# A fused retention and FFN kernel: attention units in token-pair layout, with 512-byte loads and a block-diagonal state

## The chip, the cores and the metric

The kernel runs on one core of one Trainium2 chip. The metric is the time of one execution in microseconds (us), as the device measures it. Each kernel was run several times, and one of those executions was profiled. The chips of different calls differ a little (the kernel before had medians from 327.8 to 329.8 us), so kernels are compared by ratios to runs of the kernel before on the same chip.

Engines are called PE (TensorE), PEld (its weight loads), DVE (VectorE), ACT (ScalarE), POOL (GpSimd) and SP (SyncE). SPq, ACTq and POOLq are the DMA issues of those engines.

## The reference, cut to what matters

```python
# q, k, v: (8 batches, 8 heads, 576 tokens, 64) float32; w_in (512, 2048), w_out (2048, 512)
scores = q @ k^T / 8
ret = scores * gamma_h ** (pos_q - pos_k)        # 0 where pos_k > pos_q, one gamma per head
x = (ret @ v) as (4608 tokens, 512)              # heads side by side
h = x @ w_in
g = where(h > 0, h, exp(min(h, 0)) - 1)
out = g @ w_out                                  # (4608, 512) float32
```

## The kernel before

A *unit* is 128 tokens with all eight heads; there are 36 units, nine to a pair of batches (`R = 9`). Attention is computed unit by unit. Inside a unit it is quadratic (scores, mask, AV); what earlier units of the batch contribute comes through a running state (the sum of k^T v, called `state`, and its product with q, called `inter`). The decay is folded into the factors `gk` (for v) and `gx` (for the result). The FFN works in groups of up to 512 tokens. A *slot* is one step of its stream, that is, one call of `ffn1` or `ffn2` (`ffn2` holds the matmuls with w_out). From unit 4 on, PE mixes attention units into the stream of FFN matmuls.

The parts that the change and the argument touch:

```python
def load(u, after=None):                       # one DMA of 256 KB for each of q, k, v
    ...
    for p0, b, s0, n in place(u):              # one piece of 128 tokens, or two of 64
        for dst, src in ((qk[p0:p0+n, 0], q), (qk[p0:p0+n, 1], k), (vv[p0:p0+n], v)):
            nc.sync.dma_start(dst, src[b, :, s0:s0+n, :].rearrange("h p d -> p h d"))

def state(u):                                  # own PSUM tile "st", accumulates over units
    ...
    nc.tensor.matmul(st[i*D:(i+1)*D, hp], kns[u][rows, 1, h*D:(h+1)*D], vns[u][rows, h], ...)

def state_out(u):                              # bf16 copy of the state: ACT alone
    s = ppool.tile([P, HP, D], BF16, name="sb", tag="sb")
    nc.scalar.copy(s, sts[0])

def inter(u): ...                              # 8 matmuls in 64x64 mode
def intra(u): ...                              # 8 matmuls in 128x64 mode (AV)
def stretch(u):  # one unit inside the FFN: scores(u+1), inter, state, intra, masks, put_x, state_out

def ffn1(g, ft):                               # ph = x w_in; e = exp(ph) on ACT;
    ...                                        # m = (e - 1) on POOL; g = min(max(ph,0), m) on DVE,
    late.append((slot[0], gt_, ph, m, ...))    # three slots later

# ... startup: units 0 to 3, then w_in and w_out are triggered from POOL ...
for ft in range(NFT):
    ffn1(0, ft, ...)
    if ft == 5:
        load(4, nc.vector)                     # loads of units 4 to 11
        for u in range(5, 12):
            load(u)
```

From unit 12 on, q and k are transposed by a DMA transpose that SP issues; before that PE transposes them. Full stores of the first three FFN groups are issued by ACT, later ones by SP.

Of the kernel before, what the change touches and what calls it, by code (L numbers as in the profile page):

```python
# [9 lines left out]
FP32 = mybir.dt.float32  # L10
BF16 = mybir.dt.bfloat16
I32 = mybir.dt.int32
# [5 lines left out]
def kernel(  # L18
# [9 lines left out]
    nc = tc.nc  # L28
# [18 lines left out]
    def place(u):  # L47

        pair, r = divmod(u, R)
        if r < 4:  # L50
            return [(0, 2 * pair, P * r, P)]
        if r == 4:
            return [(0, 2 * pair, 4 * P, 64), (64, 2 * pair + 1, 0, 64)]
        return [(0, 2 * pair + 1, 64 + P * (r - 5), P)]
# [17 lines left out]
    ps_st = ctx.enter_context(tc.tile_pool(name="ps_st", bufs=1, space=PSUM))  # L72
# [4 lines left out]
    def load(u, after=None):  # L77

        qk = raw.tile([P, 2, H, D], FP32, name="rqk", tag="rqk")
        vv = raw.tile([P, H, D], FP32, name="rv", tag="rv")  # L80
        if after is not None:
            after.memset(qk[0:1, 0, 0, 0:1], 0.0)
        for p0, b, s0, n in place(u):
            for dst, src in ((qk[p0 : p0 + n, 0], q), (qk[p0 : p0 + n, 1], k), (vv[p0 : p0 + n], v)):
                nc.sync.dma_start(dst, src[b, :, s0 : s0 + n, :].rearrange("h p d -> p h d"))  # L85
        raws[u] = (qk, vv)
# [16 lines left out]
    for u in range(4):  # L103
        load(u)
# [6 lines left out]
    lgk = const.tile([P, H], FP32, name="lgk")  # L111
    for h in range(H):
        nc.vector.memset(lgk[:, h : h + 1], -lg[h])
# [7 lines left out]
    pk_i = const.tile([P, R], I32, name="pk_i")  # L121
    nc.gpsimd.iota(pk_i[:, 0:4], pattern=[[P, 4]], base=-MID, channel_multiplier=1)
    nc.gpsimd.iota(pk_i[0:64, 4:5], pattern=[[0, 1]], base=4 * P - MID, channel_multiplier=1)
    nc.gpsimd.iota(pk_i[64:P, 4:5], pattern=[[0, 1]], base=-MID, channel_multiplier=1)
    nc.gpsimd.iota(pk_i[:, 5:9], pattern=[[P, 4]], base=64 - MID, channel_multiplier=1)
# [4 lines left out]
    mask = const.tile([P, 2, P], BF16, name="mask")  # L130
    nc.vector.memset(mask, 1.0)
    for m in range(2):
        nc.gpsimd.affine_select(
            out=mask[:, m], in_=mask[:, m], compare_op=ALU.is_ge, fill=0.0,
            base=0, pattern=[[1, P]], channel_multiplier=-1,
        )
    nc.vector.memset(mask[0:64, 1, 64:P], 0.0)

    pk = const.tile([P, R], FP32, name="pk")
# [3 lines left out]
    ek = const.tile([P, R, H], FP32, name="ek")  # L143
    nc.vector.tensor_tensor(
        ek,
        pk.unsqueeze(2).to_broadcast([P, R, H]),
        lgk.unsqueeze(1).to_broadcast([P, R, H]),
        ALU.mult,
    )
    gk = const.tile([P, R, H], FP32, name="gk")  # L150
    nc.scalar.activation(gk, ek, AF.Exp)
# [8 lines left out]
    qkTs, kns, vns, scs, pts, os_, sbs, sts = {}, {}, {}, {}, {}, {}, {}, {}  # L160

    def cast(u, *engs):

        rqk, _ = raws[u]
        n = nat.tile([P, 2, H * D], BF16, name="qkn", tag="qkn")
        src = rqk.rearrange("p c h d -> p c (h d)")
        if len(engs) == 1:
            engs[0](n, src)  # L168
        else:
            for c in range(2):  # L170
                engs[c](n[:, c], src[:, c])  # L171
        kns[u] = n

    def scale_v(u):
        _, rv = raws[u]
        n = nat.tile([P, H, D], BF16, name="vn", tag="vn")
        nc.gpsimd.tensor_tensor(  # L177
            n, rv, gk[:, u % R].unsqueeze(2).to_broadcast([P, H, D]), ALU.mult
        )
        vns[u] = n  # L180

    def turn(u, bank=None):
        t = tpool.tile([P, 2, HP, P], BF16, name="qkT", tag="qkT")
        n = kns[u]
        if u < PE_TURNED:
            pool, tag = bank or (ps_s, "sc")
            ps = pool.tile([P, 2, HP, P], BF16, name="tr", tag=tag)
            for c in range(2):
                for hp in range(HP):
                    nc.tensor.transpose(ps[:, c, hp], n[:, c, hp * P : (hp + 1) * P], ident)  # L190
            nc.vector.tensor_copy(t[:, 0], ps[:, 0])  # L191
            nc.scalar.copy(t[:, 1], ps[:, 1])  # L192
        else:
            nc.sync.dma_start_transpose(
                t.rearrange("p c h t -> p (c h) t"), n.rearrange("p c f -> p (c f)")
            )
        qkTs[u] = t

    def scores(u):
        t = qkTs[u]  # L200
        sc = ps_s.tile([P, 2, HP, P], FP32, name="sc", tag="sc")
        for hp in range(HP):
            for j in range(2):
                for i in range(2):
                    r = slice(i * D, (i + 1) * D)
                    nc.tensor.matmul(  # L206
                        sc[j * 64 : (j + 1) * 64, i, hp], t[r, 1, hp, j * 64 : (j + 1) * 64], t[r, 0, hp],
                        start=(hp == 0), stop=(hp == HP - 1), skip_group_check=True,
                    )
        scs[u] = sc  # L210

    def masks(u):
        pt = ppool.tile([P, 2, HP, P], BF16, name="pt", tag="pt")
        m = mask[:, 1 if u % R == 4 else 0]
        nc.vector.tensor_tensor(  # L215
            pt.rearrange("p i h t -> p (i h) t"), scs[u].rearrange("p i h t -> p (i h) t"),
            m.unsqueeze(1).to_broadcast([P, 2 * HP, P]), ALU.mult,
        )
        pts[u] = pt

    def inter(u):

        o = ps_o.tile([P, HP, P], FP32, name="o", tag="o")
        os_[u] = o
        r = u % R
        if r == 0:
            return
        n = 64 if r == 4 else P
        for hp in range(HP):
            for i in range(2):  # L230
                rows = slice(i * D, (i + 1) * D)
                nc.tensor.matmul(  # L232
                    o[rows, hp, :n], sbs[u][rows, hp], qkTs[u][rows, 0, hp, :n],
                    start=(hp == 0), stop=False, skip_group_check=True,
                )

    def state(u):

        r = u % R
        if r == 8:  # L240
            return
        if r in (0, 4):
            sts[0] = ps_st.tile([P, HP, D], FP32, name="st", tag="st")
        st = sts[0]
        rows = slice(64, P) if r == 4 else slice(0, P)
        for hp in range(HP):
            for i in range(2):
                h = 2 * hp + i
                nc.tensor.matmul(  # L249
                    st[i * D : (i + 1) * D, hp], kns[u][rows, 1, h * D : (h + 1) * D], vns[u][rows, h],  # L250
                    start=(hp == 0 and r in (0, 4)), stop=(r in (3, 7)), skip_group_check=True,
                )

    def state_out(u):
        if u % R == 8:
            return
        s = ppool.tile([P, HP, D], BF16, name="sb", tag="sb")
        nc.scalar.copy(s, sts[0])  # L258
        sbs[u + 1] = s

    def intra(u):
        o = os_[u]
        for hp in range(HP):
            for i in range(2):
                h = 2 * hp + i
                nc.tensor.matmul(  # L266
                    o[i * D : (i + 1) * D, hp], vns[u][:, h], pts[u][:, i, hp],
                    start=(u % R == 0 and hp == 0), stop=(hp == HP - 1), skip_group_check=True,
                )
# [3 lines left out]
    def put_x(u):  # L273
        g, i = group_of[u]
        if i == 0:
            xts[g] = xpool.tile([P, KJ, 512], BF16, name="xt", tag="xt")
        r = u % R
        s0 = P * r if r < 5 else 64 + P * (r - 5)
        nc.vector.tensor_tensor(  # L279
            xts[g][:, :, i * P : (i + 1) * P], os_[u], gx[:, :, s0 : s0 + P], ALU.mult  # L280
        )

    def stretch(u, ahead=True):

        ahead = ahead and u + 1 < NU
        if ahead:
            scores(u + 1)
        inter(u)
        state(u)
        intra(u)  # L290
        if ahead:
            masks(u + 1)
        put_x(u)
        state_out(u)
# [116 lines left out]
    for u in range(4):  # L411
        scores(u)
        inter(u)
        if u < 3:
            state(u)
            masks(u)
            if u == 2:
                G(seen, raws[3][0][0:1, 1, 0, 0:1])
                load_w_in(0)
                load_w_in(1)  # L420
            cast(u + 1, A, A if u == 2 else G)
            scale_v(u + 1)
            dummy(3)
            turn(u + 1, (ps_h, "ph"))
        else:
            masks(u)
            dummy(4)
            state(u)
# [113 lines left out]
```

## Time and profile before

329.34 us is the median of the first three runs (329.27 to 330.35). The profiled execution has a span of 326.0 us.

The page of the kernel before, its head. Each row of part 1 is an engine, its busy time, its share of the span, and its instructions. Then come the DMA packets by size, and the chain that ended last, by engine.

```profile
span 326.0 us, 7097 instructions
PE 312.9 (96%) x2798; PEld 162.4 (50%) x2798; DVE 186.3 (57%) x282; ACT 135.7 (42%) x243; POOL 142.9 (44%) x213
...
DMA packets 149921, 48.70 MB, mean 149 GB/s; under 512 B 138624, under 2 KB 145792, under 8 KB 149888
...
PE 81%; SPq 6%; DMA 6%; DVE 3%; POOL 2%; issue 1%; ACT 1%; ACTq 0%; DVEq 0%
```

PE is busy for 96% of the span, and the chain that ended last (the last row) is PE for 81%. The kernel is bound by matmuls for most of its time. What is not PE lies early. The view of waits of the kernel before shows two of the waits of PE ("us in total, times, longest"):

```profile
PE pmh L365 <- DMA w_out_sb<-in_moe_w_out_dram: 2.5, 2, 2.1
PE ph L320 <- DVE g L306: 1.6, 2, 1.3
```

The view of windows of the kernel before, for two stages. The columns are the stretch, its length, then busy time of PE, PEld, DVE, ACT and POOL with instruction counts, the granted PE clock, the mean DMA share and the rate.

```profile
60.00:120.00 60.00, 57.90 (x710) 34.84 (x706) 47.01 (x66) 29.91 (x56) 34.90 (x48) 1.00 1.11 210
120.00:290.00 170.00, 170.00 (x1433) 81.82 (x1433) 103.50 (x143) 70.53 (x125) 71.60 (x103) 1.00 0.63 130
```

From 120 us on PE never stops. From 60 to 120 us it is busy 57.9 of 60 us, while DVE is at 78% and the DMA engines are full (a mean share of 1.11).

One steady unit of the kernel before, from the timeline (start, us, engine, line, operation, tiles, count):

```profile
183.98 0.42 PE L206 MATMUL sc<-qkT 64*64 64x128 bf16 x16
...
184.56 0.32 PE L249 MATMUL st<-vn,qkn 128*64 128x64 bf16 x8
...
184.70 0.39 PE L266 MATMUL o<-pt,vn 128*64 128x128 bf16 x8
...
185.03 0.60 PE L320 MATMUL ph<-xt,w_in_sb 128*128 128x512 bf16 x2
```

The tiling mode of PE (the pair "64*64") changes three times around the unit: FFN to 64x64, to 128x64, and back to FFN.

### The profile page before, as it was taken

To read this page: it belongs to the slowest core of one execution; us is meant where nothing else is said; L and a number is where in the kernel's file an instruction comes from. 1 tells how busy PE (TensorE), PEld (TensorE's weight loads), DVE (VectorE), ACT (ScalarE), POOL (GpSimd) and SP (SyncE) were. 2 spreads that over 40 slices of the span, in tenths; PEclk is the share of its full clock that TensorE was granted. 3 is DMA by queue.
4 is the path that set the end of the run, shared out by engine and by line. 5 is a ranking of instruction groups with operands and counts; after the bars stand their busy time and mean duration, and the time that the engine had idled before them with its cause. 6 is when DMAs were issued, how large, how long until landed. Compare 5 with 4: busy or idle time off the path is not lost.

```text
span 326.0 us, 7097 instructions
## 1 busy us (share of the span) xinstructions
PE 312.9 (96%) x2798; PEld 162.4 (50%) x2798; DVE 186.3 (57%) x282; ACT 135.7 (42%) x243; POOL 142.9 (44%) x213
## 2 busy tenths in 40 slices
PE   8899979999979999999999999999999999999995
PEld 3444658676645454444444444444444444444442
DVE  2647604585888886666666666666666554443300
ACT  6436413555534443444444443444444443444311
POOL 3597424274646554444444444444444333333300
PEclk9999998999999999999999999999999999999999
DMA  9999999998999999887779868687724100000111
GB/s 171 214 149 200 183 230 260 226 217 200 165 232 209 213 228 180 196 171 165 163 165 156 175 135 193 151 180 164 155 67 54 45 34 32 32 34 32 64 67 64
DMA packets 149921, 48.70 MB, mean 149 GB/s; under 512 B 138624, under 2 KB 145792, under 8 KB 149888
## 3 DMA queue, kind: packets, MB, share of 16 engines
q1 hardware_dynamic: 141888, 41.96, 65.1%
q0 software_dynamic: 6272, 4.19, 8.6%
q10 hardware_dynamic: 1728, 2.10, 1.9%
q8 instruction: 22, 0.36, 0.5%
q14 instruction: 11, 0.09, 0.1%
HBM read 36.70 MB, written 9.44 MB: 142 GB/s over the span
## 4 chain that ended last, share of the span: by engine, by line
PE 81%; SPq 6%; DMA 6%; DVE 3%; POOL 2%; issue 1%; ACT 1%; ACTq 0%; DVEq 0%
PE ph L320 34%; PE pm L345 33%; SPq L85 6%; DMA rqk<-in_q_dram 4%; PE sc L206 3%; PE o L266 2%; PE o L232 2%; PE st L249 2%; DMA rv<-in_v_dram 2%; PE pmh L365 2%; PE tr L190 1%; DVE g L306 1%; DVE pt L215 1%; POOL w_out_sb L100 1%; POOL w_in_sb L95 0%
## 5 line engine op out<-in xcount | busy, mean ns | idle before, releaser
L327 POOL TENSOR_SCALAR m<-e 128x512 bf16<-128x512 f32 x144 | 90.4, 630 | 143.3 <-ACT e L325 138.6
L320 PE MATMUL ph<-xt,w_in_sb 128*128 128x512 bf16 (+1 forms) x640 | 144.5, 358 | 2.7 <-DVE g L306 1.6
L306 DVE SCALAR_TENSOR_TENSOR g<-ph,m 128x512 bf16<-128x512 f32 x144 | 98.3, 688 | 81.0 <-POOL m L327 80.7
L325 ACT ACTIVATE e<-ph 128x512 f32<-128x512 f32 x144 | 86.0, 598 | 127.7 <-PE ph L320 127.3
L345 PE MATMUL pm<-w_out_sb,g 128*128 128x512 bf16 x512 | 128.8, 379 | 0.7 <-ACT ot L356 0.7
L320 PEld LDWEIGHTS <-w_in_sb 128*128 128x128 bf16 x640 | 59.9, 98 | 63.1 <-DVE g L306 2.1
L345 PEld LDWEIGHTS <-g 128*128 128x128 bf16 x512 | 49.8, 98 | 59.4 <-issue 1.0
L215 DVE TENSOR_TENSOR pt<-sc,mask 128x1024 bf16<-128x1024 f32 x36 | 44.0, 1223 | 17.8 <-PE sc L206 17.8
L177 POOL TENSOR_TENSOR vn<-rv,gk 128x512 bf16<-128x512 f32 x36 | 38.4, 1066 | 4.1 <-DMA rv<-in_v_dram 3.5
L279 DVE TENSOR_TENSOR xt<-o,gx 128x512 bf16<-128x512 f32 x36 | 24.6, 684 | 5.5 <-PE o L266 5.5
L356 ACT COPY ot<-pm 128x512 f32<-128x512 f32 x31 | 18.2, 587 | 15.7 <-PE pm L345 15.1
L365 PE MATMUL pmh<-w_out_sb,g 128*128 128x256 bf16 x128 | 16.0, 282 | 2.5 <-DMA w_out_sb<-in_moe_w_out_dram 2.5
L168 DVE CAST qkn<-rqk 128x1024 bf16<-128x1024 f32 x24 | 18.0, 750 | 0.0
L206 PEld LDWEIGHTS <-qkT 64*64 64x64 bf16 x576 | 9.2, 106 | 15.6 <-issue 6.8
L206 PE MATMUL sc<-qkT 64*64 64x128 bf16 x576 | 15.0, 222 | 1.5 <-ACT qkT L192 1.5
L258 ACT CAST sb<-st 128x256 bf16<-128x256 f32 x32 | 11.9, 373 | 10.7 <-PE st L249 8.9
L379 PE MATMUL dum<-warm 128*128 128x512 bf16 x46 | 14.4, 448 | 1.4 <-DVE warm L108 1.3
L365 PEld LDWEIGHTS <-g 128*128 128x128 bf16 x128 | 12.7, 101 | 5.1 <-issue 2.8
L266 PE MATMUL o<-pt,vn 128*64 128x128 bf16 x288 | 14.4, 221 | 0.0
L192 ACT COPY qkT<-tr 128x512 bf16<-128x512 bf16 x12 | 7.0, 586 | 14.3 <-DVE qkT L191 14.3
L232 PE MATMUL o<-qkT,sb 64*64 64x128 bf16 (+1 forms) x256 | 12.4, 215 | 0.0
L171 POOL CAST qkn<-rqk 128x512 bf16<-128x512 f32 x10 | 6.1, 611 | 10.8 <-DMA rqk<-in_k_dram 10.8
(43 smaller groups left out, 87.6 us busy)
## 6 DMA issues: line engine op xcount, KB each, us to landing
rqk<-in_q_dram SPq DMA_DIRECT2D x32, 256.0 KB, 4.2
rqk<-in_k_dram SPq DMA_DIRECT2D x32, 256.0 KB, 4.7
rv<-in_v_dram SPq DMA_DIRECT2D x32, 256.0 KB, 4.9
out_dram<-ot SPq DMA_DIRECT2D x28, 256.0 KB, 2.3
w_in_sb<-in_moe_w_in_dram POOLq DMA_DIRECT2D x4, 512.0 KB, 7.8
w_out_sb<-in_moe_w_out_dram POOLq DMA_DIRECT2D x4, 512.0 KB, 17.5
rqk<-in_q_dram SPq DMA_DIRECT2D x8, 128.0 KB, 4.4
rqk<-in_k_dram SPq DMA_DIRECT2D x8, 128.0 KB, 4.3
```

What stands on the lines that cost most here:

```text
L85: nc.sync.dma_start(dst, src[b, :, s0 : s0 + n, :].rearrange("h p d -> p h d"))
L177: nc.gpsimd.tensor_tensor(n, rv, gk[:, u % R].unsqueeze(2).to_broadcast([P, H, D]), ALU.mult)
L206: nc.tensor.matmul(sc[j * 64 : (j + 1) * 64, i, hp], t[r, 1, hp, j * 64 : (j + 1) * 64], t[r, 0, hp], start=(hp == 0), stop=(hp == HP - 1) ...
L215: nc.vector.tensor_tensor(pt.rearrange("p i h t -> p (i h) t"), scs[u].rearrange("p i h t -> p (i h) t"), m.unsqueeze(1).to_broadcast([P, ...
L266: nc.tensor.matmul(o[i * D : (i + 1) * D, hp], vns[u][:, h], pts[u][:, i, hp], start=(u % R == 0 and hp == 0), stop=(hp == HP - 1), skip_g ...
L279: nc.vector.tensor_tensor(xts[g][:, :, i * P : (i + 1) * P], os_[u], gx[:, :, s0 : s0 + P], ALU.mult)
L306: nc.vector.scalar_tensor_tensor(gt_, ph, 0.0, m, ALU.max, ALU.min)
L320: nc.tensor.matmul(ph[:, i * n : (i + 1) * n], w_in_sb[:, j, f : f + P], xts[g][:, j, :n], start=(j == 0), stop=(j == KJ - 1), skip_group_ ...
L325: nc.scalar.activation(e, ph, AF.Exp)
L327: nc.gpsimd.tensor_scalar(m, e, -1.0, 1.0, ALU.add, ALU.mult)
L345: nc.tensor.matmul(pm, gts[g, ft][:, it * P : (it + 1) * P], w_out_sb[:, ft], start=(ft == 0), stop=(ft == NFT - 1))
L365: nc.tensor.matmul(pm, gts[g, ft][:, it * P : (it + 1) * P], w_out_sb[:, ft, c * 256 : c * 256 + 256], start=(ft == 0), stop=(ft == NFT - 1),)
```

## The change: its intent and the diff

The change puts tokens in pairs: a partition holds two neighbouring tokens of four heads. Heads 0 to 3 lie on partitions 0 to 63, heads 4 to 7 on partitions 64 to 127. A load then moves 512 contiguous bytes instead of 256. Scores, state and AV all become 64x64 quads, and the state becomes block-diagonal, so that `inter` runs on the full array in the mode of the FFN. The intent is fewer mode changes and longer DMA packets.

The price is in the details. The state shares a PSUM tile with the output `o`, each unit's part is added to a float32 running sum by DVE, and ACT and POOL each make half of the bf16 state from that sum. Casts of q and k become two instructions instead of one. Each load becomes two DMAs, one for each half of the partitions.

```diff
     def load(u, after=None, second=None):
-        for p0, b, s0, n in place(u):
-            for dst, src in (...):
-                nc.sync.dma_start(dst, src[b, :, s0 : s0 + n, :].rearrange("h p d -> p h d"))
+        for dst, src in ((qk[:, 0], q), (qk[:, 1], k), (vv, v)):
+            for hh in range(2):
+                for m0, b, s0, n in place(u):
+                    p0 = 64 * hh + m0
+                    (second or nc.sync if hh else nc.sync).dma_start(
+                        dst[p0 : p0 + n].rearrange("m j a d -> m j (a d)"),
+                        src[b, HP*hh : HP*hh + HP, s0 : s0 + 2*n, :].rearrange("j (m a) d -> m j (a d)", a=2))
 # ... constants: mask, pk, gk in the new order; nine small products for ek instead of one ...
+    nc.gpsimd.tensor_copy(mask[:, 1], mask[:, 0])
+    for p0 in (0, 64):
+        nc.vector.memset(mask[p0 : p0 + 32, 1, :, :, 32:], 0.0)
+    sbds = []                                   # three block-diagonal states, zeroed once
 # ... cast: always two instructions; scale_v: one more product in units with r == 4 ...
 # ... scores, intra, transposes: the same work as 64x64 quads ...
     def inter(u):                               # now 4 matmuls 128x128, N=128
+                    out[:, :, :n], sbds[u % 3][:, 2*hh + jp].rearrange("p i d -> p (i d)"), ...
     def state_out(u):
-        nc.scalar.copy(s, sts[0])
+        st = os_[u][:, :, P : P + D]
+        s = ppool.tile([P, HP, D], FP32, name="sum", tag="sum")
+        if r in (0, 4):
+            nc.vector.tensor_copy(s, st)
+        else:
+            nc.vector.tensor_tensor(s, st, sums[u], ALU.add)
+        nc.scalar.copy(sbds[(u + 1) % 3][:D, :, 0], s[:D])
+        nc.gpsimd.tensor_copy(sbds[(u + 1) % 3][D:, :, 1], s[D:])
     def stretch(u, ahead=True):
+        inter(u)
         if ahead:
             scores(u + 1)
-        inter(u)
         state(u)
 # ... startup: w_in(1) triggered later; state(u) before the masks, inter(u) after them ...
```

## The prediction

> **What bounds it now.** The page gives PE 96% of a 326.0 us span, and the chain of waits is 81% PE, two thirds FFN matmuls (34% and 33%). From 100 to 307 us PE never stops (windows): four N=512 matmuls take 0.86 us, and once per unit the attention inserts, by the timeline, 1.13 us (183.89 to 185.03). Before that: startup to the first FFN matmul at 21.9 us; a wait of 2.1 us at 47 us for w_out's last DMA; a bubble of 1.3 us at 96 us, where PE waits for DVE (g). DVE is 80-90% busy from 80 to 120 us. The DMA queues are saturated until about 140 us (138,624 packets under 512 B), but PE hardly waits for loads after 50 us.
>
> **PE.** Scores, state and AV keep their streamed columns: four concurrent quads per 56 ns step (trace) equal two 128x64 halves. Inter becomes four full-array matmuls of N=128, again four 56 ns steps. What goes is one change of tiling mode per unit. Before: FFN, 64x64, 128x64, FFN, three changes; after: FFN with inter, 64x64, FFN, two. [...] 90 ns between inter's last column and state's first matmul. I expect 1.02 to 1.05 us per unit, 0.1 us saved, 2.4 us over the 24 steady units and about 1 us over the others.
>
> **Loads.** Half the packets, twice the size. In startup 256 B packets flow at 218 GB/s. From the stores (1024 B in 46 ns, 2048 B in 86) I estimate 26 ns for 512 B against 18, so up to 1.3 times the rate; but each DMA now covers only 64 partitions, which may eat this. Issues double in number (estimate 0.4 us each, not 0.57).
>
> **Added.** Per unit, DVE gets a state copy/add (256 PSUM elements, like the 0.43 us half copies) and two casts of 427 ns for one of 684: +0.6 us. POOL gets a state copy of about 0.4 us. The steady stage has slack (DVE 25.5 of 40 us). Between 80 and 120 us there is none: the 96 us bubble grows by 0.5 to 1 us, and new waits for g of about 1 us appear.
> Startup: nine small ek operations instead of one delay gk, and with it gx and the first scores by about 0.5 us. State now shares PSUM with o, so state(u) waits for put_x and state_out of u-1: estimate 3.5 us per unit, not 3.27. POOL issues w_in later, so FFN starts 1 us later, and the w_out wait moves from 47 us to 48-49 us.
>
> **Sum.** PE -3.4, startup and weights +1.5, DVE stage +1.5, better loads -0.5: -0.9 us. Predicted 328.4 us, range 322.5 to 335. Faster by over 2%: 0.08; within 2%: 0.83; slower: 0.09.
>
> **What would show it.** Right: attention 1.02-1.05 us per steady unit in the timeline, period per unit 7.95 instead of 8.05 us; 55,000 fewer packets (36 units x 3 x 1024 halved); first FFN matmul at 22.5 to 23.5 us; more PE waits for DVE at 90 to 120 us. Wrong: a period unchanged or longer, or a FFN start before 21.5 us.
>
> **What would make it wrong.** DVE slower than assumed (put_x reading PSUM in pairs 64 apart[...]) would make it bind longer. Loads much faster, freeing w_out's DMA, would shorten the stage before 60 us by 2-4 us.

The PE term stands on the 90 ns of the trace. The 0.4 us an issue is an estimate, set against the 0.57 us that the trace of the kernel before shows.

## The result, and the profile after

The changed kernel is correct and takes 341.46 us (median of four runs, 339.93 to 342.33), against 329.82 us of the kernel before in the same rounds. The ratio is 1.0348, with a 95% interval from 1.0297 to 1.0398: 3.5% slower. Every ratio here is the mean time of one kernel's fast runs over that of the other's fast runs of the same rounds, so it is not quite the ratio of the medians quoted beside it.

The head of the page of the kernel after, in the same rows as before:

```profile
span 338.7 us, 8141 instructions
PE 309.3 (91%) x3174; PEld 164.4 (49%) x3214; DVE 200.0 (59%) x347; ACT 133.8 (40%) x243; POOL 163.0 (48%) x262
...
DMA packets 96550, 48.77 MB, mean 144 GB/s; under 512 B 29952, under 2 KB 92416, under 8 KB 96512
...
PE 65%; DVE 9%; DMA 7%; POOL 7%; issue 5%; SPq 3%; ACT 2%; ACTq 0%; POOLq 0%; DVEq 0%
```

PE is busy a little less (309.3 us instead of 312.9; 40 of the 3214 matmul records are missing from this trace, so the difference is rough) and the packets are as few as expected. Yet the chain that ended last is only 65% PE: DVE, POOL and "issue" have come in. The windows of the kernel after:

```profile
60.00:120.00 60.00, 51.20 (x800) 33.89 (x806) 44.22 (x69) 25.57 (x50) 33.80 (x50) 1.00 0.75 181
120.00:290.00 170.00, 164.05 (x1675) 81.59 (x1690) 114.62 (x187) 68.91 (x126) 84.20 (x127) 1.00 0.63 144
```

From 60 to 120 us PE fell from 57.9 to 51.2 us busy. No other engine is fuller than before in that stretch (DVE 44.2 us instead of 47.0), and the DMA engines fell from 1.11 to 0.75. So nothing that this view shows became saturated: engines wait for each other. (SP's DMA issues are not in this view; they come up at the end of the experiments.)

To see where the time went, follow the start of the operation `xt` (the end of the attention of a unit), which both kernels have once per unit. Start times in us in the profiled runs:

| unit | before | after | after minus before | added in this stage |
|---|---|---|---|---|
| 3 (end of startup) | 21.18 | 24.75 | +3.57 | +3.57 |
| 4 | 55.32 | 59.86 | +4.54 | +0.97 |
| 10 | 86.80 | 94.46 | +7.66 | +3.12 |
| 16 | 122.11 | 137.27 | +15.16 | +7.50 |
| 35 | 272.93 | 285.60 | +12.67 | -2.49 |

The steady stage gives 2.49 us back over 19 units, 0.13 us a unit, as predicted. It is the stage from unit 4 to 16 that costs most, 10.6 us, then startup.

The waits of the kernel after that are new or grew (the first two tiles, `sbd` and `sum`, do not exist before):

```profile
ACT sbd L304 <- DVE sum L303: 49.9, 23, 4.6
POOL sbd L305 <- DVE sum L303: 31.1, 24, 2.8
PE ph L359 <- DVE g L345: 12.0, 9, 3.7
ACT qkT L216 <- DMA rv<-in_v_dram: 3.0, 1, 3.0
DVE mask L148 <- POOL mask L146: 2.5, 1, 2.5
```

PE's wait for `g` is 12.0 us, against 1.6 before. A steady unit of the kernel after, from its timeline:

```profile
190.07 0.39 PE L259 MATMUL o<-qkT,sbd 128*128 128x128 bf16 x4
190.39 0.42 PE L232 MATMUL sc<-qkT 64*64 64x128 bf16 x16
190.64 0.29 PE L278 MATMUL o<-vn,qkn 64*64 64x64 bf16 x16
190.76 0.40 PE L289 MATMUL o<-pt,vn 64*64 64x128 bf16 x16
191.09 1.04 PE L359 MATMUL ph<-xt,w_in_sb 128*128 128x512 bf16 x3
```

The unit now has two mode changes and takes 1.02 us from its first matmul to the FFN's. Before, it took 1.05 us from its first matmul, and a mode change stood ahead of that; the prediction counted 1.13 us with this change, from 183.89 us.

### The profile page after: what moved, and what is told of

It reads as the page before. It is cut to its first block, busy times and chain, and to the rows that moved or that the text cites. A ratio compares the mean times of both kernels' runs of the same rounds, so it can differ in the third digit from the quotient of the medians.

```text
span 338.7 us, 8141 instructions
## 1 busy us (share of the span) xinstructions
PE 309.3 (91%) x3174; PEld 164.4 (49%) x3214; DVE 200.0 (59%) x347; ACT 133.8 (40%) x243; POOL 163.0 (48%) x262
## 2 busy tenths in 40 slices
DMA packets 96550, 48.77 MB, mean 144 GB/s; under 512 B 29952, under 2 KB 92416, under 8 KB 96512
## 3 DMA queue, kind: packets, MB, share of 16 engines
q10 hardware_dynamic: 2544, 2.49, 2.5%
## 4 chain that ended last, share of the span: by engine, by line
PE 65%; DVE 9%; DMA 7%; POOL 7%; issue 5%; SPq 3%; ACT 2%; ACTq 0%; POOLq 0%; DVEq 0%
PE pm L384 30%; PE ph L359 27%; POOL m L366 4%; SPq L87 3%; PE sc L232 3%; DMA rqk<-in_q_dram 2%; DMA rqk<-in_k_dram 2%; PE o L289 2%; DVE g L345 2%; DVE xt L316 2%; DVE pt L241 2%; DMA out_dram<-oth 2%; PE o L259 2%; DVE qkn L187 1%; DVE sum L303 1%
## 5 line engine op out<-in xcount | busy, mean ns | idle before, releaser
L345 DVE SCALAR_TENSOR_TENSOR g<-ph,m 128x512 bf16<-128x512 f32 x144 | 96.6, 687 | 80.2 <-POOL m L366 80.1
L366 POOL TENSOR_SCALAR m<-e 128x512 bf16<-128x512 f32 x144 | 90.7, 636 | 103.5 <-ACT e L364 96.8
L384 PE MATMUL pm<-w_out_sb,g 128*128 128x512 bf16 x502 | 127.3, 379 | 1.4 <-ACT ot L395 0.7
L364 ACT ACTIVATE e<-ph 128x512 f32<-128x512 f32 x144 | 85.3, 596 | 91.7 <-PE ph L359 84.2
L304 ACT CAST sbd<-sum 64x256 bf16<-64x256 f32 x32 | 12.9, 404 | 64.9 <-DVE sum L303 49.9
L305 POOL CAST sbd<-sum 64x256 bf16<-64x256 f32 x32 | 12.8, 398 | 45.3 <-DVE sum L303 31.1
L187 DVE CAST qkn<-rqk 128x512 bf16<-128x512 f32 x49 | 22.5, 499 | 0.3 <-DMA rqk<-in_k_dram 0.3
L289 PE MATMUL o<-pt,vn 64*64 64x128 bf16 x576 | 14.6, 220 | 0.8 <-DVE pt L241 0.8
L404 PE MATMUL pmh<-w_out_sb,g 128*128 128x256 bf16 x128 | 14.8, 273 | 0.5 <-DVE g L345 0.5
L259 PEld LDWEIGHTS <-sbd 128*128 128x128 bf16 x128 | 9.5, 98 | 6.2
L259 PE MATMUL o<-qkT,sbd 128*128 128x128 bf16 (+1 forms) x128 | 11.9, 216 | 0.0
```

Of the source, the lines that this page charges most:

```text
L187: engs[c % len(engs)](n[:, c], rqk[:, c].rearrange("p j a d -> p a j d"))
L259: nc.tensor.matmul(out[:, :, :n], sbds[u % 3][:, 2 * hh + jp].rearrange("p i d -> p (i d)"), qkTs[u][:, 0, :, jp, hh * 64 : hh * 64 + n], ...
L345: nc.vector.scalar_tensor_tensor(gt_, ph, 0.0, m, ALU.max, ALU.min)
L364: nc.scalar.activation(e, ph, AF.Exp)
L366: nc.gpsimd.tensor_scalar(m, e, -1.0, 1.0, ALU.add, ALU.mult)
L384: nc.tensor.matmul(pm, gts[g, ft][:, it * P : (it + 1) * P], w_out_sb[:, ft], start=(ft == 0), stop=(ft == NFT - 1))
```

## The experiments

Eighteen kernels were run. All are correct, except e6, which gives a wrong result. Each of them was profiled. The table gives medians, ratios to the kernel before on the same chip, and the start of `xt` of units 3, 4, 10 and 16.

| run | what | median us | ratio (95%) | u3 | u4 | u10 | u16 |
|---|---|---|---|---|---|---|---|
| before | | 329.82 | 1 | 21.2 | 55.3 | 86.8 | 122.1 |
| after | | 341.46 | 1.0348 | 24.8 | 59.9 | 94.5 | 137.3 |
| e1_defer | after, state copies 2 slots later | 339.57 | 1.0306 (1.0277 to 1.0336) | 24.8 | 59.8 | 94.1 | 136.6 |
| e2_sp_stores | after, all stores from SP | 356.81 | 1.0817 (1.0763 to 1.0870) | 25.2 | 78.4 | 112.9 | 154.4 |
| e3_const | after, constants reordered | 339.62 | 1.0314 (1.0268 to 1.0359) | 22.0 | 57.5 | 94.4 | 135.4 |
| e4_wissue | after, weights triggered earlier | 337.31 | 1.0243 (1.0205 to 1.0282) | 23.9 | 60.8 | 92.8 | 133.8 |
| e5_scores_first | after, two more mode changes | 344.16 | 1.0479 (1.0417 to 1.0542) | 23.9 | 60.9 | 93.0 | 135.9 |
| e6_load128 | after, loads into 128 partitions | 347.4 (one run) | not timed | 24.7 | 70.9 | 102.9 | 143.9 |
| e7_b_dve | before, DVE work of the change | 329.13 | 0.9997 (0.9967 to 1.0028) | 21.9 | 54.3 | 85.8 | 123.2 |
| e8_b_coupled | before, work and coupling | 337.16 | 1.0245 (1.0209 to 1.0281) | 22.5 | 58.0 | 90.4 | 131.1 |
| e10_defer_sp | e1, full stores from SP | 335.09 | 1.0170 (1.0133 to 1.0207) | 23.9 | 61.0 | 93.0 | 131.5 |
| e11_all | e10 + e3 + e4 | 331.30 | 1.0044 (0.9992 to 1.0095) | 22.7 | 59.9 | 91.8 | 130.3 |
| e12_cast_va | e11, casts on DVE and ACT | 331.12 | 1.0071 (1.0022 to 1.0120) | 22.4 | 56.4 | 89.7 | 127.3 |
| e13_state_late | e12, state after transposes | 330.77 | 1.0066 (1.0012 to 1.0120) | 22.4 | 58.1 | 90.6 | 126.7 |
| e14_loads_late | e13, loads at slot 12 | 333.63 | 1.0124 (1.0075 to 1.0173) | 22.8 | 53.6 | 88.5 | 130.4 |
| e15_b_loads_late | before, loads at slot 12 | 324.58 | 0.9867 (0.9840 to 0.9895) | 21.1 | 51.1 | 82.8 | 118.1 |
| e16_loads_mid | e13, loads at slot 9 | 332.45 | 1.0098 (1.0052 to 1.0145) | 22.6 | 53.5 | 86.8 | 129.1 |
| e17_b_loads_mid | before, loads at slot 9 | 324.64 | 0.9850 (0.9801 to 0.9899) | 21.4 | 52.8 | 84.3 | 119.6 |
| e18_b_head_halves | e15, loads in two halves of heads | 331.73 | 1.0090 (1.0022 to 1.0158) | 21.8 | 53.0 | 85.3 | 126.8 |
| e19_b_part_halves | e15, loads in two halves of partitions | 340.15 | 1.0362 (1.0297 to 1.0427) | 21.5 | 50.9 | 90.7 | 133.0 |

### DVE's work, or what waits for DVE? (e7, e8, e1)

The theory after the result was head-of-line blocking. In the trace of the kernel after ACT and POOL take their work in program order: 257 operations and DMA issues of ACT, and 238 of POOL, start in the order of the program. Each has a copy of the state that needs DVE's `sum`, and DVE reaches `sum` only after its masks and `xt` (masks at 108.28 us, `xt` at 109.42, `sum` at 110.02). Until then ACT cannot do the `e` of the next FFN slot, and POOL cannot do its `m`. The timeline of the kernel after shows it:

```profile
110.02 0.41 DVE L303 TENSOR_TENSOR sum<-o,sum 128x256 f32<-128x256 f32 x1
...
110.46 0.41 ACT L304 CAST sbd<-sum 64x256 bf16<-64x256 f32 x1 [4.25 <-DVE sum L303]
110.77 1.07 ACT L364 ACTIVATE e<-ph 128x512 f32<-128x512 f32 x2
111.08 0.59 PE L359 MATMUL ph<-xt,w_in_sb 128*128 128x512 bf16 x2 [1.08 <-DVE g L345]
```

ACT stood 4.25 us (the number in brackets) for `sum`, then made two `e` at once. PE waited 1.08 us for a free `ph` bank, which `g` frees. The rival was the prediction's own reason: DVE simply has more to do. Two kernels were built from the kernel *before* to part the two.

e7 adds the DVE work alone:

```diff
-        if len(engs) == 1: engs[0](n, src)
-        else: ...
+        for c in range(2):
+            engs[c % len(engs)](n[:, c], src[:, c])
 # state_out
+        w = ppool.tile([P, HP, D], FP32, name="sum", tag="sum")
+        nc.vector.tensor_copy(w, os_[u][:, :, :D])          # nobody reads it
         nc.scalar.copy(s, sts[0])
```

> The kernel before, with the DVE work that the change adds and nothing else of it: every cast as two of 512, and one more DVE copy of 256 PSUM columns per unit (of o, to a tile that nobody reads). Rival B (DVE work): at least 5 us more between the xt of units 10 and 16 (35.3 us before). Theory A: the work alone costs at most 2 us there, and the kernel stays within 1% of before (329.8 us).

e8 adds the same work, but ACT and POOL read its result:

```diff
 # state_out
-        nc.scalar.copy(s, sts[0])
+        w = ppool.tile([P, HP, D], FP32, name="sum", tag="sum")
+        nc.vector.tensor_copy(w, sts[0])
+        nc.scalar.copy(s[:D], w[:D])
+        nc.gpsimd.tensor_copy(s[D:], w[D:])
```

> As the run before it (DVE work added to the kernel before), but the DVE copy is of the state's PSUM, and the bf16 state is made from it by ACT (64 partitions) and POOL (64 partitions), so both queues wait for DVE once per unit, as in the changed kernel. Theory A: 3 us or more above the run with the DVE work alone, lost between units 10 and 16. Rival B: within 1 us of that run.

e7 took 329.13 us, ratio 0.9997: the work costs nothing in the whole. From unit 10 to 16 it cost 2.1 us (37.4 us instead of 35.3), but unit 4 had come 1.0 us earlier than in the kernel before. e8 took 337.16 us, ratio 1.0245, 8 us more. The waits of e8 have the pattern of the kernel after:

```profile
ACT sb L257 <- DVE sum L255: 64.2, 32, 4.6
POOL sb L258 <- DVE sum L255: 44.7, 32, 6.6
```

So the coupling is shown to be costly, and DVE's added busy time is not. One thing more differs between e7 and e8: POOL has a copy of 0.40 us a unit to make, and no run takes that out alone. It does not fill POOL, which is busy for 34.4 us from 60 to 120 us in e8 and for 33.7 in e7. Part of e8's 8 us lies before unit 4 (+2.7 us): there POOL's copy also stands ahead of the triggers of the weights, as in the kernel after, where POOL waited 2.68 us for `sum` before them (below).

The cure in the kernel after is to do the copies two FFN slots later, when `sum` is ready:

```diff
 # state_out, units from 5 on
-        nc.scalar.copy(sbds[(u + 1) % 3][:D, :, 0], s[:D])
-        nc.gpsimd.tensor_copy(sbds[(u + 1) % 3][D:, :, 1], s[D:])
+        owed.append((slot[0], u))               # settled in tick(), two slots later
```

> The changed kernel, with the ScalarE and GpSimd copies of the state (sbd<-sum) put two FFN slots later in their queues from unit 5 on; the work is the same. Theory A (head of the line): these copies wait for DVE's sum and keep the FFN's exp (e) and m behind them in ACT's and POOL's queues; between the xt of units 10 and 16 the change took 42.8 us instead of 35.3. If A holds, this stretch falls by 3 us or more and the time from 341.5 to 336-338 us. Rival B (DVE has simply too much work there): the DVE work is unchanged, so under 1 us is gained. Rival C (ACT waits in front of its store issues for recycled DMA semaphores): under 1 us from this edit.

e1 took 339.57 us. From 60 to 130 us its waits for `sum` fell from 21.4 to 3.0 us on ACT and from 18.1 to 6.6 us on POOL, but it gained at most about 2 us (the intervals of the two ratios overlap), and from unit 10 to 16 hardly anything (42.5 us instead of 42.8). My expectation for that stretch was missed. Other waits stood there in its place: PE stood 2.2 us at 121 us for a deferred copy on POOL, and ACT stood before a store. The second led to the next experiments.

### ACT's stores that wait for loads (e2, e10)

The ACT engine's timeline of the kernel after, with its idle time in brackets:

```profile
82.11 0.59 ACT L395 COPY ot<-pm 128x512 f32<-128x512 f32 x1 [0.21 <-PE pm L384]
85.36 0.34 ACTq L396 DMA_DIRECT2D out_dram<-ot  x1
85.74 0.59 ACT L216 COPY qkT<-tr 128x512 bf16<-128x512 bf16 x1 [3.04 <-DMA rv<-in_v_dram]
```

ACT finished `ot` at 82.70 us and issued its store only at 85.36 us. The store needs nothing but `ot`. What ended the wait, by the trace, was the landing of a load of v, with which the store shares no data. The records of the trace show the link. The 304 DMAs of SP and ACT signal eight completion semaphores, 38 each (184 DMAs and 23 each in the kernel before). Ahead of this store, the first of the four full stores on ACT, ACT has an instruction that waits for the semaphore which the store will use. The last DMA on it was a load of v, issued at 81.83 us; it landed at 85.28 us, and the wait ended at 85.30. So the wait stands in the program. The kernel before has waits of the same kind: ahead of a half store ACT stood from 44.61 us until a load of q had landed at 48.13. A late load so holds up ACT, and with it `e` and the FFN: behind this one PE waited 1.44 us for `qkT` (at 86.38 us).

e2 moves all of those stores to SP:

```diff
-            (nc.scalar if g < 3 else nc.sync).dma_start(out[...], ot)
+            nc.sync.dma_start(out[...], ot)
-        nc.scalar.dma_start(out[u * P ...], ot)             # the half stores of group 0
+        nc.sync.dma_start(out[u * P ...], ot)
```

> The changed kernel, with all stores issued from SP's queue, none from ACT's. Theory C: in the changed kernel ACT stood for 2.6 us before a store issue at 85.4 us and 1.8 us before one at 119.4 us, each ended by the completion of a load (rv) that had used the same completion semaphore; twice as many loads make the semaphores come round faster. If C holds, the PE gaps at 64, 84.5 us (1.5 and 1.6 us) vanish and the time falls by 2-4 us. If C is wrong, nothing changes, or the stores now hold up the loads behind them in SP's queue and it gets slower.

e2 was a miss: 356.81 us. Unit 4 came at 78.4 us, 18.5 us later than in the kernel after. The eight half stores of group 0 now stood in SP's queue behind the loads of units 4 to 11. SP issued loads until 74.9 us and only then the stores:

```profile
73.66 1.25 SPq L87 DMA_DIRECT2D rv<-in_v_dram  x2
75.01 8.86 SPq L410 DMA_DIRECT2D out_dram<-oth  x8
```

Until then no buffer for a further `oth` came free: ACT waited 23.0 us and DVE 21.0 us for the landing of such a store. The stage from 10 to 16 fell to 41.5 us, so the idea was not refuted, only its execution. e10 leaves the half stores on ACT and moves only the full stores of groups 1 and 2, with the deferral of e1:

> The changed kernel with two edits: the ACT and POOL state copies two FFN slots later (as the first experiment, which alone gained 2 us or less), and the four full stores of groups 1 and 2 issued from SP instead of ACT (the half stores of group 0 stay on ACT, as moving those cost 20 us). In the first experiment ACT still stood 2.7 us before the store issue at 118.8 us. Theories A and C together: with both waits gone the xt of units 10 to 16 take 38-39 us (42.8 in the change, 42.5 with the first edit alone, 37.4 with the DVE work alone), and the time is 334-337 us. If DVE work is the rest, this stretch stays above 41 us.

e10 took 335.09 us, ratio 1.0170. From 10 to 16 it took 38.5 us instead of 42.8, and ACT's waits for loads are gone from that stretch. Deferral alone gave 0.3 us there (e1), moved stores alone 1.3 us (e2, with the half stores moved too), both together 4.3 us: each of the two waits hides the other.

### Startup: constants and the order on POOL (e3, e4)

The constants of the kernel after, from the timeline:

```profile
5.01 0.27 DVE L148 MEMSET mask<- 32x64 uint32 x2 [2.48 <-POOL mask L146]
...
5.75 0.78 DVE L156 TENSOR_TENSOR ek<-pk,lgk 128x8 f32<-128x8 f32 x9
...
6.56 0.26 ACT L163 ACTIVATE gk<-ek 128x72 f32<-128x72 f32 x1 [2.39 <-DVE ek L156]
```

In the prediction I charged the nine small `ek` operations with a delay of 0.5 us. They cost 0.78 us together, 0.55 more than the one before (0.23 us). What matters is the row above: DVE waited 2.48 us at a memset of the mask for POOL, and the position data `pk`, `ek` and `gk` stood behind it. `gk` started at 6.56 us; before, it did at 3.85. e3 puts the memset after `ek` (and POOL's zeroing of the states ahead of POOL's copy in `gk`):

```diff
-    for p0 in (0, 64):
-        nc.vector.memset(mask[p0 : p0 + 32, 1, :, :, 32:], 0.0)
     pk = const.tile([P, R, 2], FP32, name="pk")
 # ... after gk:
+    for p0 in (0, 64):
+        nc.vector.memset(mask[p0 : p0 + 32, 1, :, :, 32:], 0.0)
+    # the zeroing of sbd follows here
```

> The changed kernel with its constants in another order: DVE's memset of the mask's second half, which stood for 2.5 us in front of pk, px and ek until POOL had made the mask, comes after ek; POOL's memsets of the state tiles come before the copy of gk. Theory D: the late first scores (10.9 us instead of 9.45) come from this wait in DVE's queue, not from the nine ek operations (0.8 us) alone. If D holds, gk is ready near 4.5 us (6.6 before the edit), the first scores start at 9.3 to 9.7 us, and the time falls by 1-1.5 us. If the ek operations were the cause, the first scores stay above 10.3 us.

With e3 the first scores start at 9.28 us (10.90 after, 9.45 before) and the first FFN matmul at 22.69 us (25.54 after, 21.92 before). So 2.85 us of the late start are this order. In the total at most 1 to 2 us remain (ratio 1.0314 instead of 1.0348, with intervals that overlap), because the stages behind took the rest back: unit 10 came at 94.44 us, as in the kernel after.

The triggers of the weights stand on POOL, behind its copy of the state of unit 3. The kernel after, from the timeline:

```profile
25.91 0.40 POOL L305 CAST sbd<-sum 64x256 bf16<-64x256 f32 x1 [2.68 <-DVE sum L303]
26.36 1.48 POOL L100 DMA_DIRECT2D w_in_sb<-in_moe_w_in_dram  x2
...
27.83 3.53 POOL L105 DMA_DIRECT2D w_out_sb<-in_moe_w_out_dram  x4
...
31.43 0.62 POOL L366 TENSOR_SCALAR m<-e 128x512 bf16<-128x512 f32 x1
```

POOL waited for `sum`, then triggered weights for 5.0 us, and only then made the first `m`. FFN had started at 25.54 us, and PE stood 3.7 us for `g` (the "longest" of the row "PE ph <- DVE g" above). Behind this wait the granted clock was low too: 0.83 from 30 to 40 us, where the kernel before has 1.00. e4 triggers before the copy:

```diff
         put_x(u)
+        if u == 3:
+            for n in range(2, 4): load_w_in(n)
+            for n in range(4): load_w_out(n)
         state_out(u)
```

> The changed kernel with POOL's last six weight loads (two of w_in, four of w_out; about 5 us of POOL time) issued before the copy of unit 3's state instead of after it, as that copy waits for DVE. Theory E: this wait pushes the issues into the time when the first FFN groups need POOL for m; PE stands 3.8 us at 28.8 us for it (0.5 us before). If E holds, that gap falls below 1 us. What is gained in the end is 1.5 to 3.3 us; less than the gap if PE then waits for w_out, as the kernel before did at 47 us. If E is wrong, the gap stays.

e4 took 337.31 us. PE's wait for `g` fell to 0.2 us, but it had to wait 2.9 us for w_out at 48 us, as the kernel before did (2.5 us in all). So before unit 4 nothing was gained: the prediction had the wait for w_out right in kind. The ratio is 1% lower than that of the kernel after; this was gained behind unit 4 (unit 10 at 92.84 us instead of 94.46, unit 16 at 133.83 instead of 137.27), and I have not followed it further.

### Everything together (e11, e12, e13)

e11 is e10 with e3 and e4.

> The four edits together (state copies later, full stores on SP, constants in order, weights before unit 3's state copy). If the causes found add up, about 12 us come back less some overlap: 329-332 us, near the kernel before (329.5), with a steady period of 7.93 us per unit. If they are not the causes, it stays above 335 us.

It took 331.30 us, ratio 1.0044 (0.9992 to 1.0095), the same as the kernel before within the error. Four changes of order, with the layout, the matmuls and the loads untouched, took back nearly all of the 3.5%. e12 lets ACT take half of the casts (`prep(u + 3, V, A)` for `prep(u + 3, V)`), e13 puts the state matmuls of startup after the transposes of the next unit:

```diff
         scores(u)
-        state(u, first=True)
 # ... masks, cast, scale, turn(u + 1) ...
+        state(u, first=True)
         inter(u)
```

> The four edits together, and one of the two casts of units 12 on given to ACT instead of DVE. What the earlier run with four edits still loses between units 10 and 16 (38.5 us against 35.3 before) should be the DVE work that the change added; it is 37.4 in the kernel before with that work alone. If so, this stretch falls to 36-37 us and the time by 1.5-2.5 us, to 329-330 us. If not, it stays at 38.5.

> As the run before it, and in the startup the state matmuls of units 0 to 3 are issued after the transposes of the next unit instead of right after the scores, so that PE does not stand for DVE's reads of the shared PSUM tile (0.4 us each at 16 and 20 us in the run with four edits). Expected: FFN starts 0.8-1.5 us earlier than there (23.5 us) and the time is 1 us lower than the run before it: 328-329.5 us, level with the kernel before. If w_out's last DMA then holds PE (as it did at 47 us), half of that is lost again.

e12 took 331.12 us and e13 330.77 us. Both stayed short of what I had expected, and neither differs from e11 by more than the intervals (ratios 1.0071 and 1.0066 against 1.0044). e13's own edit did not do what it was for: its first FFN matmul starts at 23.18 us, in e12 at 23.11. The stretch from unit 10 to 16 is 36.0 us in e13, near the 35.3 us of the kernel before, but unit 4 came 2.8 us later than before.

### Mode changes and the DMA's partitions (e5, e6)

e5 puts scores ahead of inter, so that the modes change four times a unit instead of two:

```diff
-        inter(u)
         if ahead:
             scores(u + 1)
+        inter(u)
```

> The changed kernel with one thing swapped in the steady part: scores before inter, so that the order of tiling modes per unit is full array (FFN), 64x64, full array, 64x64, full array: four changes of mode instead of two. Theory F: the shorter steady period of the change (7.93 us per unit, 8.05 before) comes from the number of mode changes, about 0.09-0.11 us each. If it holds, the period becomes 8.10-8.15 us and the time rises by 4-5 us. If the gain came from elsewhere (fewer inter matmuls, say), the period stays at 7.93.

From unit 16 to 35 e5 took 152.25 us, the kernel after 148.33: 0.21 us a unit for two more changes, about 0.1 us each. This agrees with what the prediction took from the trace (90 ns).

e6 loads with 512-byte elements into all 128 partitions. Its result is wrong (it reads other tokens), so it only times the transfers:

```diff
-        for dst, src in (...):
-            for hh in range(2):
-                for m0, b, s0, n in place(u): ...     # 64 partitions each
+        for c, (dst, src) in enumerate(((qk[:, 0], q), (qk[:, 1], k), (vv, v))):
+            h0 = HP * ((u + c) % 2)
+            nc.sync.dma_start(dst.rearrange("m j a d -> m j (a d)"),
+                src[b, h0 : h0 + HP, s0 : s0 + 2 * P, :].rearrange("j (m a) d -> m j (a d)", a=2))
```

> A wrong result on purpose: the changed kernel, but each load of q, k or v is one transfer of 512-byte pieces into all 128 partitions (of other rows of the same tensors), as many bytes as before, half as many transfers. In the change the startup loads run at 212 GB/s, no faster than the 256-byte ones before (218). Theory G: the halves on 64 partitions are the cause; then this run shows 250 GB/s or more at 5-15 us. Rival: something else (the reading side, say) holds 512-byte pieces at that rate; then it stays at 205-225 GB/s. The time itself should move by 1-3 us at most either way, as startup does not wait for loads; if ACT's waits before stores shrink with half as many transfers, up to 4 us faster.

The packets of 512 B then flow faster. In the view of windows, 6 to 13 us (the settled part of startup) has 276 GB/s in e6, 211 in the kernel after, and 218 in the kernel before, whose packets are half the size. So on 64 partitions the longer packets gave nothing. (e6 also halves the number of transfers, so it alone does not part the two; e18 and e19 do, below.) These rates don't show why.

The total of e6, 347.4 us in one run of unknown state, was no gain, and this was not expected. Its waits from 48 to 70 us:

```profile
ACT oth L409 <- DMA rqk<-in_q_dram: 11.1, 1, 11.1
...
PE pmh L404 <- ACT oth L409: 6.2, 1, 6.2
```

ACT stood 11.1 us until a load of q had landed, before a half store. This is a wait of the kind that e10 had taken away for the full stores. Why it was so long in e6 was not followed.

### What is left before unit 4: loads beside w_out (e14, e15)

In e13 the loads of units 4 to 11 move beside w_out, and PE waited 1.5 us for w_out at 47 us. e14 is e13 with the loads triggered at FFN slot 12 instead of 5. e15 is the same edit in the kernel before:

```diff
-        if ft == 5:
+        if ft == 12:
             load(4, nc.vector)
```

> The kernel of run e13_state_late with the q, k, v loads of units 4 to 11 triggered seven FFN slots later (slot 12 instead of slot 5), so that they no longer move beside w_out. Theory C (the time still lost before unit 4 is w_out sharing the DMA queues with the 512-byte loads): PE's wait for w_out near 47 us (1.7 to 2.6 us in the runs so far) goes to under 0.5 us, unit 4 starts 1 to 2.5 us earlier than its 58.1 us, total 328 to 329.5. Rival (w_out is late because it is issued late, or the loads are themselves what unit 4 waits for): the wait for w_out stays above 1.5 us, or PE waits as long for the loads of unit 4; total 330.5 to 333.

> The kernel before with the same delay of the loads of units 4 to 11. Theory C: the kernel before loses little to this contention (its loads have 256-byte elements and w_out was issued earlier), so within 1 us of the kernel before, 328 to 330. Rival (contention costs both kernels alike): 326.5 to 328, and then the delay says nothing on the change.

Half of each expectation came true, and both totals fell outside what either theory gave (e14 just above, e15 below). The wait for w_out vanished in both, and unit 4 came 4.6 us earlier in e14 and 4.2 us in e15. So contention with w_out costs both kernels alike. The trace of the kernel before shows the loss. From 32 to 40 us, loads and weights have almost the same number of packets (1904 and 1971; 976 each from 36 to 40 us), and the weights get 123 GB/s from 36 to 40 us where they had 196 from 28 to 32 us, almost alone. Why the counts are equal no run shows.

e15 kept its gain: 324.58 us, ratio 0.9867, faster than both kernels. e14 lost more than it had won. From unit 4 to 16 it took 76.9 us (e13: 68.5), with PE waiting 4.0 us for `qkT` and POOL up to 4.3 us for a load of v. In the kernel before, loads triggered that late were early enough. In the changed one they were not. e16 and e17 trigger at slot 9, between the two:

> e13_state_late with the loads of units 4 to 11 triggered at slot 9, between slot 5 (e13: PE waits 1.5 us for w_out, unit 4 at 58.1 us, units 4 to 16 take 68.5) and slot 12 (e14: no wait for w_out, unit 4 at 53.6, units 4 to 16 take 76.9 because POOL and PE then wait for loads). If the 64-partition loads are what is short after 80 us in the changed kernel, each us gained before unit 4 is given back there: unit 4 at 54 to 56, units 4 to 16 72 to 75 us, total 330 to 333. If the late loads of e14 were only a matter of those few us: unit 4 at 54 to 56, units 4 to 16 68 to 70, total 326.5 to 328.5.

> The kernel before with the loads of units 4 to 11 at slot 9. With slot 12 (e15) it gained all of 4.2 us and waited for no load after. If contention with w_out alone set those 4.2 us, slot 9 gives part to all of it: unit 4 at 51 to 53 us, units 4 to 16 67 us, total 324.5 to 327, not faster than e15.

e16 took 332.45 us, and 75.65 us from unit 4 to 16, close to what the theory of scarce loads said (72 to 75). e17 took 324.64 us, and 66.79 us for the same units, as the kernel before. So once its loads are not started early, the changed kernel is short of loads.

### Why loads are short: the number of issues (e18, e19)

The q1 row (loads) of the DMA view of 58 to 84 us, one fence each for the kernel before and the kernel after. Its columns are packets, MB, and the time that the packets took as a share of 16 DMA engines:

```profile
q1 hardware_dynamic: 20190, 5.08, 96.4%
```

```profile
q1 hardware_dynamic: 9110, 4.39, 61.1%
```

The kernel after moves less (4.39 MB instead of 5.08) with DMA engines that this queue keeps busy for only 61.1%; e14 has 4.56 MB and 63.2%. What is full is the issuing engine. SP's timeline in the kernel after:

```profile
69.49 1.26 SPq L87 DMA_DIRECT2D rqk<-in_q_dram  x2
70.79 1.27 SPq L87 DMA_DIRECT2D rqk<-in_k_dram  x2
72.17 1.25 SPq L87 DMA_DIRECT2D rv<-in_v_dram  x2
...
94.69 1.35 SPq L218 DMA_TRANSPOSE qkT<-qkn  x1
```

From 62 to 94 us SP issues almost without a pause, 1.26 us for the two halves, and a new pair begins every 1.34 us on average ((72.17 - 69.49)/2). An estimate from this: 262,144 bytes in 1.34 us are 196 GB/s, the most that SP asks for at this pace. In units that straddle two batches there are four issues a tensor, of half the size, which took 1.81 to 2.94 us. The kernel before needs one issue a tensor. From 138 to 192 us those of q and k took 0.57 to 0.64 us and those of v 0.73 to 2.75; from 58 to 73 us, where loads fill the DMA engines (the 96.4% above), all took 0.86 to 1.81 us. SP also issues the transposes of units from 12 on. The first one left at 84.16 us in the kernel before, and at 94.69 us in the kernel after, behind its load issues (the kernel after as a whole was 7.7 us late at unit 10, so this alone is no proof).

Two causes remained: the doubled number of issues, or the 64 partitions of each transfer. e18 doubles the issues in e15 and keeps 128 partitions; e19 halves the partitions:

```diff
 # e18, units from 4 on
-                nc.sync.dma_start(dst, src[b, :, s0 : s0 + n, :]...)
+                for h0, h1 in ((0, HP), (HP, H)):
+                    nc.sync.dma_start(dst[:, h0:h1], src[b, h0:h1, s0 : s0 + n, :]...)
 # e19, units from 4 on: the pieces (p0, n) split at partition 64, all eight heads in each
```

> The kernel of e15_b_loads_late (kernel before, loads of units 4 to 11 at slot 12; 324.6 us, no engine waits long for loads) with each load of units 4 to 35 issued as two transfers of four heads each, still 128 partitions and 256-byte elements: twice as many issues, nothing else. Theory I (in the changed kernel SP issues loads back to back at 1.25 us a pair from 60 to 90 us while the DMA engines are 61 to 63% busy, so the doubled issues set the rate of the loads): SP issues back to back here too, loads move 4.4 to 4.7 MB in 58 to 84 us instead of 5.1, engines below 90%, POOL or PE wait for loads by 80 to 100 us, units 4 to 16 take 70 to 76 us instead of 67.05, total 327 to 333. Theory P (it is the 64 partitions of each transfer): an issue then costs about half of 0.6 to 0.9 us, the rate stays at 5 MB, total 323.5 to 325.5.

> e15_b_loads_late with each load of units 4 to 35 issued as two transfers of 64 partitions each, all eight heads, still 256-byte elements: the same number of issues as e18 and as the changed kernel, and its halves of the partitions. Theory I: like e18, total 327 to 333. Theory P: here and not in e18 the rate falls (4.4 to 4.7 MB in 58 to 84 us) and the total rises by 3 us or more. Both at once: slower than e18 by 2 us or more.

e18 took 331.73 us, ratio 1.0090 against e15's 0.9867, so about 7 us for twice the issues. e19 took 340.15 us, ratio 1.0362, 8 to 9 us more again. Both causes are real. SP's timeline in e18:

```profile
69.53 1.00 SPq L86 DMA_DIRECT2D rv<-in_v_dram  x2
...
86.31 1.27 SPq L86 DMA_DIRECT2D rv<-in_v_dram  x2
...
91.16 1.47 SPq L195 DMA_TRANSPOSE qkT<-qkn  x1
```

The first transpose left at 91.16 us (83.49 in e15, while unit 10 was only 2.5 us later), and PE waited 4.3 us for it. What stood before it were the loads of unit 13, which straddles two batches: its pieces have 64 partitions, and twelve issues were needed, in pairs of 1.25 to 1.37 us (one pair took 2.24). From 77 to 90 us SP issued without a pause, while loads kept the DMA engines busy for 52.8% only. This is theory I as it was put down, except that the loads of 58 to 84 us were 4.87 MB, more than the 4.4 to 4.7 expected.

In e19 a pair took 1.27 to 1.31 us nearly all along, and 3.99 MB moved in that window. Here SP also stood from 72.1 to 76.5 us, so not all of the shortfall is issuing. An issue for 64 partitions thus took 0.63 us in the kernel after, in e19 and in unit 13 of e18, and one of the same bytes for 128 partitions some 0.5 us in the other units of e18. Why is open. It is not the number of elements: 256 in an issue of the kernel after (0.63 us), 512 in one of e18 (0.5 us) and of e6 (0.37 to 0.50 us from 69 to 76 us).

One more thing made these waits dear. After the wait of 4.3 us the granted clock in e18 was 0.73 from 90 to 100 us, where e15 has 1.00; in e19 it was 0.71 after a wait of 6.2 us. So the totals of e18 and e19 hold the wait and a slower PE behind it, and I did not part the two.

A single DMA for both halves of the partitions, which would remove both causes, did not build, so it was not run. So no version of this layout beat the kernel before.

## Why the prediction was right or wrong

The prediction was 328.4 us with a chance of 0.83 for no change. The result is 341.46 us, 3.5% slower and above the range of 322.5 to 335 us. Its sum was PE -3.4, startup and weights +1.5, DVE stage +1.5, loads -0.5. Measured in the same terms:

- **PE: right.** The steady unit takes 1.02 us (1.02 to 1.05 predicted), its period is 7.93 us (7.95 predicted), and units 16 to 35 gave back 2.49 us (2.4 predicted for 24 units). e5 shows by a reversal that it is the mode changes (0.21 us a unit for two more). The further 1 us in the other units could not show, because PE waited there.
- **Packets: right in number, and it did not matter.** 53,371 packets fewer (149,921 to 96,550; 55,000 predicted). By the two rows of the DMA view above a packet took 27.9 ns instead of 19.9 on average (share of busy time, times 16 engines and 26 us, over packets), so the estimate of 26 and 18 ns was near. "Each DMA now covers only 64 partitions, which may eat this" was right: e6 (276 GB/s against 211 in startup), and e19 against e18 (340.15 us against 331.73).
- **Issues: the step "estimate 0.4 us each, not 0.57" failed.** They take 0.63 us each. Their number doubled and their time did not fall, so SP needs 1.25 us for what took one issue before. I had noted the number and never asked what share of SP's time it is. From 62 to 94 us SP hardly has a pause, and the first transpose waits behind its loads. e18 shows that the doubled issues alone cost about 7 us where the loads are not started early. In the change as it stood, with loads at slot 5, their part is smaller, because e11 to e13 keep all the issues and come within 0.7% of the kernel before. I can't give its share there.
- **Startup and weights, +1.5: the mechanisms were half right, the sizes wrong.** It was +4.5 us by unit 4. The late `gk` was not the nine operations (+0.55 us) but a memset in DVE's queue that waited 2.48 us for POOL (e3 got 2.85 us of FFN start back). "State(u) waits, 3.5 us per unit" was right: 3.46 us (24.75 minus 14.38 for three units; 3.14 before). "POOL issues w_in later" was right in kind; it cost a wait of 3.7 us for `g` and a lower clock behind it (0.83), not a shift of 1 us. "The w_out wait moves to 48-49 us" was right once that wait was gone (e4).
- **DVE stage, +1.5: the step "there is none [slack]: the 96 us bubble grows by 0.5 to 1 us" failed, and it is the largest error.** Units 4 to 16 cost 10.6 us more. I had added DVE's busy time and asked whether DVE becomes full. e7 shows that this work is free in the total. What costs is the order: two other engines wait in their own queues for DVE's result (e8: +8 us in the kernel before, 2.7 of them before unit 4), and ACT waits for loads before its stores (e10: 4.0 us in units 10 to 16 beyond e1).
- **Conditions named as dangers.** Slower `put_x` was none: 684 ns before and after. The casts took 419 ns (427 assumed). "Loads much faster, freeing w_out's DMA" did not happen, but the amount named there, 2 to 4 us, is about what e15 gained by moving the loads out of w_out's way (unit 4 came 4.2 us earlier). That is luck, not foresight.

What stays open: how the loss of the change divides exactly between coupling, ACT's store waits and load issues. They hide one another (e1 alone 2 us, e10 6 us, e11 10 us), so single numbers don't add up. Also open is the longer issue for 64 partitions.

## What to carry to other kernels

When a change lets two engines read what a third engine makes, do not add the new busy time to the third: look at what stands behind the new read in the queues of the two (here ACT stood 4.25 us for one such read, with two `e` behind it), and put the read a few slots later. When a layout splits a transfer, count issues of the queue's engine as work of an engine (here 1.26 us a pair, begun every 1.34 us), and look at what else that engine must issue behind them; half as many packets were worth nothing here with twice as many issues on half the partitions. Before tuning loads further, check whether they move beside a weight that is needed sooner: here a later trigger, one number, gained 1.3 to 1.5% in the kernel before.
